# Two groups of unread products in the begin of an attention and two-layer kernel, where there were five

## The chip, the core and the metric

The kernel runs on one core of a Trainium2 chip. The metric is the device time of one execution in microseconds (us); smaller is better. The engines named below are TensorE (PE in the rows; PEld is its weight load), VectorE (DVE), ScalarE (ACT), GpSimd (POOL) and SyncE (SP), whose queue issues the loads and stores.

## The reference

Inputs are q, k, v of shape (4, 8, 768, 64), eight memory keys and values for each of the 32 heads, and four weight matrices. Attention goes by chunks of 32 queries: each chunk sees the 8 memory keys, 16 keys to the left of it, its own 32 and 8 to the right, 64 in all. The heads are then joined to 3072 tokens of 512 features, and two layers follow:

```python
scores = scale * np.matmul(q_c, k_full.transpose(0, 1, 3, 2))
a = np.exp(scores - max); a = a / (sum + 1e-09)
x = np.matmul(a, v_full)              # joined to (3072, 512)
h = x @ w_in;  g = h * np.clip(h + 3.0, 0.0, 6.0) / 6.0;  x = g @ w_out
h = x @ w_in2; g = np.maximum(0.01 * h, h);               out = g @ w_out2
```

Both layers have 2048 hidden features. The weights come as 64-bit floats and are decoded on the chip.

## The kernel before

**Arithmetic.** A float32 product is made from three products of a coarse float32r part and a remainder: coarse by coarse, remainder by coarse, coarse by remainder. So each operand is split once: ACT casts the coarse part (recorded as line 341), DVE subtracts it for the remainder (recorded as line 344).

**The begin.** The first block of 512 tokens needs the attention of two whole units of work, (0, 0) and (0, 1), which are 384 tokens by half the heads each, and of two half units, (1, 0, 0) and (1, 1, 0). One unit is a chain that goes from engine to engine: SP loads queries, keys and values; ACT, DVE or POOL copies the keys into windows (lines 525 and 795) and POOL the memory values (lines 517 and 789); PE makes the scores (line 544, halves 811); DVE finds the greatest (561 and 563, halves 825 to 834); ACT makes exponentials (580, halves 845); DVE sums and normalises (598, halves 862); PE transposes (602, halves 866); ACT copies the transposed weights back (recorded as 341); PE makes the values (622, halves 882 and 894); ACT and DVE split the result into xh and xl. Then come the products of the first layer, `hidden` (line 998) and `output` (line 1047), in groups of 12 products of 128x512, with half units (1, 0, 1) and (1, 1, 1) and later units between them. Beside all this the weights are decoded: ACT (396), then DVE (400, 404, 408), then split as above.

**Unread products.** `warm` (line 454) issues products of the identity matrix into a corner of a PSUM bank that no instruction reads. Each of its products shows as two records in the trace.

```python
def warm(n, after=None, home=None):
    b, c = home or Buf("ac"), 2 if home else 4
    def fn(e):
        x = made(b)[:, 1, N - 128 * c:].rearrange("p (a n) -> p a n", a=c)
        for _ in range(n):
            nc.tensor.matmul(x, ident, ident.unsqueeze(1).to_broadcast([128, c, 128]), start=True, stop=True, skip_group_check=True)
    add(fn, {"PE": c * n * (220.0 if after else 430.0)}, after.key + 0.5 if after else -200.0, after=[after] if after else [], allocs=[] if home else [b], uses=[home] if home else [], ins=4 * n)
```

Four groups stand among the first scores (lines 1560 to 1563). Line 1565 adds five more, each released by a mark: ("s", ...) is the scores of a unit, ("t", ...) its transposes, ("v", ...) its values. They write 256 columns each (128x256 in the rows) into `home`, the bank "ac" of the half unit (1, 1, 0). The exponentials of that half unit read the same bank, and instructions on one bank are kept in their order.

**The order of the work.** Nothing is written in the order in which it runs. A planner, `schedule` (line 103), holds a time for each engine and picks, whenever one is free, the ready task with the lowest key; the cost that a task names is the planner's time for it. The order that it finds is the program order of each engine's queue, and an engine takes its queue in order. For a group of two products with a home, the planner's PE cost is 2 x 2 x 220 = 880 ns, and its key lies 0.5 after that of its mark: -77.5, -86.5, -80.5, -68.5 and -67.5 for the five groups, against -80 for the values of unit (0, 0), -81 for the transposes of (0, 1), -74 for the values of (0, 1) and -68 and -62 for those of the half units.

**The loads.** SP issues loads in program order, at most eight outstanding; a ninth waits for the landing of the first (the kernel's planner counts the same eight, line 92). A load also waits until its buffer is free.

Of the kernel before, what the change touches and what calls it, by code (L numbers as in the profile page):

```python
# [255 lines left out]
def tile_attn_moe_moe2(ctx: ExitStack, tc: tile.TileContext, raw, w1i, w1o, w2i, w2o, out):  # L256
# [197 lines left out]
# [10 lines that stand above are left out]
# [1098 lines left out]
    warm(2, marks["s", 0, 1])  # L1562
    warm(1, marks["s", 1, 0, 0])
    home = marks["b", 1, 1, 0][0]
    for m, n in ((("s", 1, 1, 0), 2), (("t", 0, 0), 3), (("t", 0, 1), 3), (("t", 1, 1, 0), 2), (("v", 1, 0, 0), 2)):
        warm(n, marks[m], home)
    for u in range(2):
        half_unit(1, u, 1, -20.0 + 6.0 * u, "at", LOADS[4 + u], "ACT", 1.0)
# [45 lines left out]
    for kind, j, f, *n in seq2:  # L1614
        if kind == "p":
            p, i, n = j, f, n[0]
# [69 lines left out]
```

## Time and profile before

| | us |
|---|---|
| median of 3 runs | 1044.6 (1043.4 to 1045.1) |
| the profiled execution, its own time | 1042.63 |
| its span, first to last instruction | 1040.9 |
| PE busy | 1030.1 |
| DVE busy | 855.1 |
| ACT busy | 692.6 |

The profile is of one execution; 1.7 us of its time lie outside the span. A row of a timeline gives the start and the duration of merged neighbours on one engine, the line, the operation, what is written from what, the count, and in brackets the idle time ahead of it with what ended it.

### The profile page before, as it was taken

The numbers are of one execution on the slowest core, as the hardware profiler recorded it, in microseconds if no ns is written. First come the engines' busy times: TensorE is split into PE (matmuls) and PEld (weight loads), VectorE is DVE, ScalarE is ACT, GpSimd is POOL, SyncE is SP. The second block draws the span as 40 slices with busy tenths as digits, with TensorE's granted clock in tenths as the row PEclk, the third lists the DMA queues.
The fourth block names the chain that finished last, engine by engine and source line by source line (L and its number), as shares of the span: only waits on it lengthen the run. The fifth ranks groups of instructions, "written<-read, shape, count | busy, mean of one in ns | idle before, by whom it ended". The sixth has DMA issues, their size and how long they took to land.

```text
span 1040.9 us, 20153 instructions
## 1 busy us (share of the span) xinstructions
PE 1030.1 (99%) x7476; PEld 849.9 (82%) x7476; DVE 855.1 (82%) x1423; ACT 692.6 (67%) x1478; POOL 22.3 (2%) x30
## 2 busy tenths in 40 slices
PE   7999999999999999999999999999999999999998
PEld 4788988888888888888888888888888888888887
DVE  6896897578999887599999898999466998566775
ACT  4896776656888554576786576775565874666753
POOL 4010000000000000000000000000000000000000
PEclk9999999999999999999999999999999999999999
DMA  9889787887897989464638894456342564522451
GB/s 266 297 241 324 258 281 238 254 293 221 286 315 232 328 280 322 157 214 135 215 129 281 268 299 151 152 170 204 128 156 81 182 200 143 179 105 99 144 182 61
DMA packets 127315, 220.50 MB, mean 212 GB/s; under 512 B 12528, under 2 KB 76016, under 8 KB 127216
## 3 DMA queue, kind: packets, MB, share of 16 engines
q1 hardware_dynamic: 127216, 219.20, 63.1%
q8 instruction: 59, 0.97, 0.4%
q14 instruction: 40, 0.33, 0.1%
HBM read 156.24 MB, written 62.91 MB: 211 GB/s over the span
## 4 chain that ended last, share of the span: by engine, by line
PE 96%; DMA 1%; DVE 1%; ACT 1%; issue 0%; SPq 0%; ACTq 0%; DVEq 0%
PE y L1322 17%; PE y L1047 15%; PE y L1490 13%; PE h L1322 11%; PE h L1490 8%; PE hx L1490 8%; PE hx L1322 8%; PE h L998 8%; PE h L1047 2%; PE at L634 2%; DMA w<-in_raw 1%; PE at L544 1%; PE at L602 1%; PE ac L461 1%; ACT w L845 0%; PE at L622 0%
## 5 line engine op out<-in xcount | busy, mean ns | idle before, releaser
L344 DVE TENSOR_TENSOR w<-w 128x512 fp32r<-128x512 f32 (+2 forms) x407 | 333.4, 858 | 28.6 <-ACT w L341 28.2
L341 ACT CAST w<-w 128x512 fp32r<-128x512 f32 (+1 forms) x296 | 226.5, 799 | 16.6 <-DMA w<-floats 7.2
L1322 PE MATMUL y<-w 128*128 128x512 f32 x516 | 124.5, 390 | 0.0
L1047 PE MATMUL y<-g,w 128*128 128x512 f32 (+1 forms) x540 | 124.4, 374 | 0.0
L1322 PEld LDWEIGHTS y<-w 128*128 128x128 f32 x516 | 96.7, 188 | 19.9
L1047 PEld LDWEIGHTS y<-g,w 128*128 128x128 f32 x540 | 94.2, 189 | 17.3
L341 ACT CAST g<-w 128x512 fp32r<-128x512 f32 x80 | 49.7, 622 | 67.6 <-PE y L1490 22.3
L1490 PE MATMUL y<-w 128*128 128x512 f32 x384 | 90.3, 389 | 0.0
L1490 PEld LDWEIGHTS y<-w 128*128 128x128 f32 x384 | 72.1, 188 | 14.9
L1296 ACT ACTIVATE w<-w 128x512 f32<-128x512 f32 x72 | 45.2, 631 | 43.0 <-DVE w L1289 21.5
L344 DVE TENSOR_TENSOR g<-w,g 128x512 fp32r<-128x512 f32 x80 | 54.8, 694 | 14.6 <-ACT g L341 14.4
L998 PE MATMUL h<-xh,w 128*128 128x512 f32 (+1 forms) x288 | 66.0, 370 | 0.0
L1490 PE MATMUL h<-w 128*128 128x512 f32 x264 | 62.1, 389 | 0.0
L1490 PE MATMUL hx<-w 128*128 128x512 f32 x252 | 59.2, 389 | 0.0
L1322 PE MATMUL h<-xl,w 128*128 128x512 f32 x240 | 58.2, 390 | 0.0
L1490 PEld LDWEIGHTS h<-w 128*128 128x128 f32 x264 | 49.6, 188 | 10.2
L998 PEld LDWEIGHTS h<-xh,w 128*128 128x128 f32 x288 | 49.7, 189 | 8.9
L1490 PEld LDWEIGHTS hx<-w 128*128 128x128 f32 x252 | 47.3, 188 | 9.8
L1322 PEld LDWEIGHTS h<-xl,w 128*128 128x128 f32 x240 | 44.9, 188 | 9.3
L1322 PE MATMUL y<-xh,w 128*128 128x512 f32 x216 | 52.0, 390 | 0.0
L1367 DVE TENSOR_TENSOR w<-y,w 128x512 f32<-128x512 f32 x35 | 24.0, 691 | 29.7 <-PE y L1322 26.9
L1322 PEld LDWEIGHTS y<-xh,w 128*128 128x128 f32 x216 | 40.5, 188 | 8.4
(243 smaller groups left out, 1836.5 us busy)
## 6 DMA issues: line engine op xcount, KB each, us to landing
w<-kept2i SPq DMA_DIRECT2D x42, 512.0 KB
w<-kept2o SPq DMA_DIRECT2D x42, 512.0 KB
w<-kept1i SPq DMA_DIRECT2D x28, 512.0 KB
a<-in_raw SPq DMA_DIRECT2D x20, 448.0 KB
w<-in_w1i SPq DMA_DIRECT2D x16, 512.0 KB
w<-in_w1o SPq DMA_DIRECT2D x16, 512.0 KB
w<-in_w2i SPq DMA_DIRECT2D x16, 512.0 KB
w<-in_w2o SPq DMA_DIRECT2D x16, 512.0 KB
```

Source lines behind the costliest of these rows:

```text
L341: nc.scalar.copy(out, in_) if e == "ACT" else engine(e).tensor_copy(out=out, in_=in_)
L344: engine(e).tensor_tensor(out=out, in0=a, in1=b, op=ALU.subtract)
L461: nc.tensor.matmul(x, ident, ident.unsqueeze(1).to_broadcast([128, c, 128]), start=True, stop=True, skip_group_check=True)
L544: nc.tensor.matmul(ps.t[h * CHUNK:(h + 1) * CHUNK, par, i * W:(i + 1) * W], qk[h // 2].t[r, gp, (h % 2) * G + c * CHUNK:(h % 2) * G + (c + ...
L602: nc.tensor.transpose(pt.t[:, i // NC, (i % NC) * 128:(i % NC + 1) * 128], pview()[:, i * 128:(i + 1) * 128], ident)
L634: nc.tensor.matmul(pv.t[(h % 2) * D:(h % 2 + 1) * D, par, (h // 2) * 2 * G + i * CHUNK:(h // 2) * 2 * G + (i + 1) * CHUNK], v[h // 2].t[r, ...
L998: nc.tensor.matmul(h.t[:, o:o + n], w.t[:, 1 if p == 1 else 0, k * 128:(k + 1) * 128], x[:, k, c0:c0 + n], start=(p == 0 and k == 0 and o ...
L1047: nc.tensor.matmul(bank(banks[d])[:, c0:c0 + n], w.t[:, 1 if p == 1 else 0, d * 128:(d + 1) * 128], g.t[:, 1 if p == 2 else 0, at:at + n], ...
L1296: return add(lambda e: nc.scalar.activation(out=at(), in_=at(), func=AF.Prelu, alpha=0.01), {"ACT": act(N)}, key, after=[after], uses=uses)
L1322: nc.tensor.matmul(bank(to), wt(l, o)[:, kt * 128:(kt + 1) * 128].bitcast(F32R), operand(p, name, 1 if q == 2 else 0, kt).bitcast(F32R), s ...
L1367: done[2] = add(lambda e: nc.vector.tensor_tensor(out=half_of(x, 0), in0=bank(bb), in1=ut.t[:, 0], op=ALU.add), low, key, after=[k, done[1 ...
L1490: nc.tensor.matmul(bank(to[d]), wt(1 if q == 1 else 0, o)[:, d * 128:(d + 1) * 128].bitcast(F32R), g.t[:, 1 if q == 2 else 0], start=(fres ...
```

## The change

It takes three of the five groups of line 1565 out: the one behind the scores of half unit (1, 1, 0), the one behind its transposes, and the one behind the values of half unit (1, 0, 0). The two behind the transposes of the whole units stay, three products each.

```diff
-    for m, n in ((("s", 1, 1, 0), 2), (("t", 0, 0), 3), (("t", 0, 1), 3), (("t", 1, 1, 0), 2), (("v", 1, 0, 0), 2)):
+    for m, n in ((("t", 0, 0), 3), (("t", 0, 1), 3), ):
         warm(n, marks[m], home)
```

## Rows read from the trace of the kernel before

**Rows 1.** The page, part 1: busy us (share of the span) and instructions.
```profile
PE 1030.1 (99%) x7476; PEld 849.9 (82%) x7476; DVE 855.1 (82%) x1423; ACT 692.6 (67%) x1478; POOL 22.3 (2%) x30
```
**Rows 2.** Waits of PE over the span: in total, times, longest, us.
```profile
PE ac L461 <- ACT w L845: 2.0, 1, 2.0
...
PE at L602 <- DVE w L598: 1.2, 2, 0.9
```
**Rows 3.** Timeline of PE, 17 to 45 us: start, us, work, idle before.
```profile
17.50 0.84 PE L602 MATMUL at<-ident,w 128*128 128x128 f32 x6 [0.25 <-DVE w L598]
18.94 1.56 PE L461 MATMUL ac<-ident 128*128 128x256 f32 x6 [0.59 <-DVE mx L825]
22.47 1.13 PE L461 MATMUL ac<-ident 128*128 128x256 f32 x4 [1.97 <-ACT w L845]
23.53 2.92 PE L622 MATMUL at<-w 64*64 64x32 f32 x96
26.38 1.54 PE L602 MATMUL ab<-ident,w 128*128 128x128 f32 x6
27.72 2.77 PE L461 MATMUL ac<-ident 128*128 128x256 f32 x6
...
31.13 1.78 PE L622 MATMUL ab<-w 64*64 64x32 f32 x96
32.84 1.13 PE L461 MATMUL ac<-ident 128*128 128x256 f32 x4
...
34.81 1.13 PE L461 MATMUL ac<-ident 128*128 128x256 f32 x4
35.87 0.98 PE L882 MATMUL ac<-w 64*64 64x32 f32 x48
36.78 0.72 PE L811 MATMUL at<-w 64*32 64x64 f32 x48
37.44 2.11 PE L998 MATMUL h<-xh,w 128*128 128x512 f32 x8
...
44.34 1.14 PE L894 MATMUL at<-w 64*64 64x32 f32 x48 [0.61 <-ACT w L341]
```
**Rows 4.** Windows: length, busy us of PE, PEld, DVE, ACT, POOL, granted clock, DMA.
```profile
20.50:22.47 1.97, 0.00 (x1) 0.00 (x1) 1.71 (x3) 1.93 (x13) 1.89 (x2) 1.00 0.73 180
23.36:38.39 15.03, 15.03 (x368) 12.85 (x367) 11.72 (x29) 9.14 (x30) 2.88 (x4) 0.77 0.83 277
23.65:30.48 6.83, 6.83 (x109) 6.09 (x110) 5.41 (x10) 2.30 (x6) 2.59 (x4) 0.50 0.96 368
...
38.39:78.00 39.61, 38.96 (x398) 31.37 (x397) 39.15 (x80) 36.94 (x118) 2.97 (x2) 1.00 0.84 266
45.41:1037.30 991.89, 990.94 (x6726) 822.86 (x6723) 822.55 (x1337) 664.88 (x1378) 11.31 (x7) 1.00 0.63 210
```
**Rows 5.** Timeline of ACT, 18 to 62 us.
```profile
18.88 0.78 ACT L341 COPY w<-at 128x768 f32<-128x768 f32 x1
20.54 0.31 ACT L845 ACTIVATE w<-ac,mx 128x64 f32<-128x64 f32 x1 [0.88 <-PE ac L461]
...
35.42 1.14 ACT L341 COPY w<-w 128x336 f32<-128x336 f32 x4
...
61.51 2.23 ACT L341 COPY w<-w 128x336 f32<-128x336 f32 x8 [0.78 <-DMA w<-in_raw]
```
**Rows 6.** Timeline of DVE, 23 to 39 us: its two idle stretches.
```profile
27.58 1.15 DVE L344 TENSOR_TENSOR xl<-at,xh 128x256 fp32r<-128x256 f32 x4 [1.42 <-ACT xh L341]
...
32.42 0.43 DVE L400 TENSOR_SCALAR wm<-wm 128x512 uint32<-128x512 uint32 x1 [1.89 <-ACT wm L396]
```
**Rows 7.** Timeline of POOL, 14 to 16 us.
```profile
14.21 1.27 POOL L341 COPY w<-w 8x768 f32<-8x768 f32 x2 [1.88 <-DMA w<-in_raw]
```
**Rows 8.** Timeline of SP's queue, 33 to 34 us.
```profile
33.36 0.27 SPq L787 DMA_DIRECT2D w<-in_raw  x1
33.76 0.40 SPq L769 DMA_DIRECT2D w<-in_raw  x1
```

## The prediction, made before the changed kernel was run

> **What bounds the kernel now.** I read the page first. PE is busy for 1030.1 of 1040.9 us [rows 1], so the kernel is a chain of products with some 10 us of holes, and a change to a few products can only matter by what PE waits for or by how fast it runs. The waits of PE come next [rows 2]: its longest wait is one of 2.0 us, of an unread product (line 461) for the exponentials of line 845. After the begin there is next to nothing: from 45.41 us to the end PE idles 0.95 us (the last line of that group) [rows 4], one wait for the normalisation. So whatever the change does, it does before 45 us, and the rest follows as a block, sooner or later by what the begin gives.
>
> The timeline of PE through the begin [rows 3] shows where the groups stand. The six records at 18.94 us are the group behind the transposes of unit (0, 0), which stays. The four at 22.47 are the first group that goes. The six at 27.72 stay. The four at 32.84 and the four at 34.81 go. Between 23.53 and 43 us PE has no hole at all. That looks like a PE bound, but part of the work in it is unread, and part of it is slow: the table of stretches gives a granted clock of 0.50 from 23.65 to 30.48 us [rows 4], the lower of the two levels, 1.2 GHz instead of 2.4. It fell after PE had done nothing for 1.97 us (20.50 to 22.47).
>
> DVE is the other engine to watch. From 23.36 to 38.39 us it is busy for 11.72 of 15.03 us, so 3.31 us of it are idle, and from 38.39 to 78 us it is busy for 39.15 of 39.61 [rows 4]. Its two holes are of 1.42 and 1.89 us, and sum to just those 3.31 [rows 6]: the first waits for the split of unit (0, 0)'s values, the second for a decode that stands on ACT behind the copy of transposed weights. Both are late because PE is late.
>
> **The change part by part.** *The group at 22.47 us.* The values of unit (0, 0) follow it at 23.53. Their inputs are there long before: ACT has the transposed weights copied at 18.88 + 0.78 = 19.66 us [rows 5], POOL has the memory values of that unit at 14.21 + 1.27 = 15.48 [rows 7]. The group that stays ends at 20.50. So the values can begin at 20.5 instead of 23.53: 3.03 us, of which 1.97 are the wait and 1.06 the products. The group waits because the exponentials read the same bank from 20.54 on [rows 5], and everything behind it on PE's queue waits with it.
>
> *The slow stretch.* If PE goes on at 20.5 without a hole, the work of 23.53 to 30.48 runs at 2.4 GHz. The same 96 products of values take 2.92 us there and 1.78 us at 31.13; six transposes 1.54 against 0.84 at 17.50; six unread records 2.77 against 1.56 at 18.94 [rows 3]. That is 1.14 + 0.70 + 1.21 = 3.05 us.
>
> *The groups at 32.84 and 34.81 us.* They cost 1.13 us each, 2.26 together [rows 3], and the values of the half units come that much sooner.
>
> On PE alone that makes 3.03 + 3.05 + 2.26 = 8.3 us: the values of the second half unit would end at 28.5 instead of 35.87 + 0.98 = 36.85. But PE is not alone. The scores of half unit (1, 0, 1) at 36.78 need the key windows that ACT copies at 35.42 [rows 5], behind casts that wait for DVE; the first-layer products at 37.44 need the remainders of DVE. DVE can close its 3.31 us of holes and no more, since from 23.36 on it has that work before it whatever PE does, and it has no holes behind. ACT is busy for 9.14 of the same 15.03 us and follows. So the begin comes 3.3 us sooner, and the other 5 us turn into idle time of PE, between 28.5 and about 35.42 + 1.14 - 3.3 = 33.2 us: 4.7 us in which it has nothing to do.
>
> *What that idle time does to the clock.* After 1.97 us without work the clock fell [rows 4]; here are 4.7, and no unread product is left in them. I expect it to fall again. No row shows the price, so I bound it: nothing if it does not fall; 6.83 / 2 = 3.41 us if a stretch as long as the one in the trace lies wholly on first-layer products, which are on the path. A gain by the clock is excluded, because the real products behind run at full clock already. I take a stretch of that same length that starts halfway through the idle time, at 30.9 us: it ends at 37.7, has 4.5 us of real products in it, and costs half of that, 2.2 us.
>
> *The planner.* Three tasks of 880 ns leave its PE, and it may order later work otherwise. The nearest row says how little there is to lose or win, the 0.95 us that PE idles in all the rest [rows 4]; I take 0 and keep 1 us either way.
>
> The sum is -3.3 + 2.2 = **-1.1 us**. The profiled execution took 1042.63 us, 1.73 of them outside its span, and the sum says 1041.5 for it. It is 2.0 us below the median of the runs shown, 1044.6, to which I apply the same difference: **1043.5 us**. About 0.2%, 2.1 us, is what a measurement of this kernel can tell from no change, so my forecast is none that can be told.
>
> **A rule weighed against this.** Rows 4 show one fall of the clock in one execution, with its place. The Trainium skill, page "TensorE: Matmul & The Clock Gate", section "Part 1: The HAM clock gate", says that how many products run at the lower clock varies from run to run of the same kernel. By that rule the slow stretch of 23.65 us need not be in every execution of the kernel before, and the 3.05 us need not be there to win: the last rival below. The three times shown, all above the profiled one, neither show nor exclude it.
>
> **The rivals.**
>
> *The clock holds.* PE's idle time is shorter than I think, or cut up by the small products of the half units, and the clock stays at 2.4 GHz. For it: the hole of 0.59 us at 18.94 [rows 3] brought no fall, the clock stands at 1.00 behind it [rows 4]. Against it: the hole of 1.97 us brought one. Then the whole 3.3 us come through: 1044.6 - 3.3 = 1041.3 us.
>
> *The loads don't follow.* What SP issues behind 33.36 us is paced by landings: the next load of queries and keys goes out at 33.76, only 0.40 us later [rows 8], so an earlier free buffer moves it by at most 0.4 us. At 61.51 us ACT already waits 0.78 us for such a load [rows 5]; were everything else 3.3 us sooner, it would wait 4 us there, with casts that PE needs behind it. DVE and ACT are both over 93% busy in that stretch and could not make it up. Then 0.4 us are left: 1044.2 us. Against it: PE may have enough prepared work to bridge part of that wait, and the planner would put the copies later.
>
> *The fall moves from unread products to real ones (slower).* In executions of the kernel before without the slow stretch, its begin would already be 3.05 us sooner than in the profile, since PE's work up to 36.85 us, which DVE waits for, shrinks by that. The change can then win only 3.31 - 3.05 = 0.26 us, and pays for the fall that its idle time brings, 2.2 to 3.4 us: slower by 2.0 to 3.1, I take 2.5, 1047.1 us. It decides from the point where most executions of before lack the stretch and those of after have one on the first-layer products. For it: the group at 22.47 ends a hole, and the two at 32.84 and 34.81 fill just the place where the new hole would be. Against it: the only execution that can be seen has the stretch and is the fastest of the four times.
>
> *The change does nothing.* Unread products would be free if what follows them were not ready. At 22.47 us it is ready by 3 us, so I give this nothing of its own.
>
> **How the numbers follow.** My forecast, a gain partly paid back by the clock, gets 0.44; its bounds are 1041.3 and 1044.7. The clock holds: 0.22. The loads don't follow: 0.14. The fall moves to real products: 0.20. Faster by over 0.2% is the second case and the edge of the first, 0.22 + 0.03 = 0.25. Slower by over 0.2% is the last case without its mild end, 0.19. Within 0.2% is the rest, 0.56. The range goes from 1040.9, the second case with 0.4 for the planner, to 1047.0, near the middle of the last case; about 1 in 10 is left out above and less below.
>
> **What would show it.** In the timeline of PE the values of unit (0, 0) begin at 20.5 us right behind six unread records; the exponentials of line 845 no longer hold PE. In the stretches DVE is busy without a hole from 23.4 us to the scores of half unit (1, 0, 1), which come at about 33.5 instead of 36.78. PE idles some 4 us just before them, and the granted clock falls there and comes back among the products of line 998. The values at 44.34 us [rows 3] come 1 to 2 us sooner. I am wrong if the clock stays up through 29 to 40 us (then 3.3 us sooner), if PE has new waits between 45 and 80 us that end on ACT or a load (then the loads decide), or if the values of unit (0, 0) still begin at 23.5.

## The result, and the profile after

The changed kernel takes 1050.06 us (median of 6 runs, 1048.43 to 1051.58), the kernel before 1044.42 (6 runs, 1043.40 to 1046.29). The ratio is 1.0051, 95% interval 1.0038 to 1.0065: slower by 5.3 us, where no change was forecast and 1047.0 was the top of the range. Run again later it was slower by 0.41% (experiment 7). The profiled execution took 1048.93 us, its span 1047.2.

The page of the changed kernel, first lines:

```profile
span 1047.2 us, 20144 instructions
## 1 busy us (share of the span) xinstructions
PE 1028.2 (98%) x7464; PEld 845.8 (81%) x7464; DVE 854.1 (82%) x1421; ACT 694.0 (66%) x1478; POOL 24.8 (2%) x32
```

PE is busy for 1.9 us less than in [rows 1], and the span is 6.3 us longer. So 8 us more are idle. Where? Part of it is in the begin, as expected. The timeline of PE there, which answers to [rows 3]:

```profile
18.90 1.56 PE L461 MATMUL ac<-ident 128*128 128x256 f32 x6 [0.59 <-DVE mx L825]
20.39 0.82 PE L622 MATMUL at<-w 64*64 64x32 f32 x35
21.53 1.24 PE L622 MATMUL at<-w 64*64 64x32 f32 x61 [0.31 <-issue]
...
27.84 0.69 PE L882 MATMUL ac<-w 64*64 64x32 f32 x30
32.35 0.80 PE L882 MATMUL ac<-w 64*64 64x32 f32 x18 [3.82 <-issue]
34.24 1.46 PE L811 MATMUL at<-w 64*32 64x64 f32 x48 [1.09 <-ACT w L341]
35.63 3.14 PE L998 MATMUL h<-xh,w 128*128 128x512 f32 x8
```

The values of unit (0, 0) begin at 20.39, right behind the group that stays. Then PE stops for 3.82 us in the middle of the values of the second half unit, 30 records in, and waits for nothing that the profile shows ("issue"). A second wait, of 1.09 us, is for ACT. ACT makes the key windows of half unit (1, 0, 1) there, which it made at 35.42 in [rows 5]; the timelines of ACT and of SP's queue in the changed kernel:

```profile
33.58 1.11 ACT L341 COPY w<-w 128x336 f32<-128x336 f32 x4 [2.29 <-DMA w<-in_raw]
```

```profile
33.58 0.27 SPq L787 DMA_DIRECT2D w<-in_raw  x1
```

ACT had waited 2.29 us for the load of that half unit's queries and keys (line 769). The same landing lets SP's ninth load go, the row of SP; in the kernel before that row stands at 33.36 [rows 8]. So the load is no sooner than before, and it bounds the begin: the scores of (1, 0, 1) come 0.66 us behind the start of the copy, at 34.24 instead of 36.78. The copy begins as this load lands in experiments 1, 3, 5, 6 and 7 too (at 34.45, 33.16, 34.47, 33.47 and 33.70 us), and the scores 0.65 to 0.66 us behind it.

The first-layer products begin at 35.63 instead of 37.44. The scores before them take 1.46 us instead of 0.72, and the first eight products 3.14 instead of 2.11. The stretches of the changed kernel, columns as in [rows 4], say why these are slow, and where the rest of the time is:

```profile
28.53:32.35 3.82, 0.00 (x1) 0.00 (x0) 3.82 (x13) 1.82 (x7) 0.00 (x0) 0.83 0.99 317
31.03:37.86 6.83, 4.33 (x71) 3.37 (x71) 5.73 (x19) 4.49 (x18) 0.00 (x0) 0.50 0.68 184
...
45.00:1035.00 990.00, 983.44 (x6681) 814.10 (x6680) 819.11 (x1332) 664.94 (x1376) 13.95 (x9) 1.00 0.63 210
110.00:120.00 10.00, 8.13 (x125) 7.11 (x125) 9.97 (x18) 8.80 (x29) 1.65 (x1) 1.00 0.52 157
120.00:180.00 60.00, 56.79 (x923) 46.23 (x916) 50.46 (x99) 43.28 (x152) 3.04 (x2) 1.00 0.85 268
```

The clock stands at 0.50 from 31.03 to 37.86 us, on the scores and the first-layer products. But the larger part is behind the begin: from 45 to 1035 us PE idles 990.00 - 983.44 = 6.56 us, where the kernel before idles 0.95; 1.87 of it between 110 and 120 us, 3.21 between 120 and 180. The waits of PE behind 45 us in the changed kernel (total, times, longest):

```profile
PE at L544 <- issue: 2.3, 3, 1.8
PE y L1047 <- ACT g L341: 1.5, 1, 1.5
PE at L634 <- ACT a L341: 0.7, 1, 0.7
PE at L602 <- DVE w L598: 0.7, 1, 0.7
```

The kind of the last one is in [rows 2], but at another place (208.98 us there, 131.47 here); the others are not. They are of instructions that the change does not touch, in the attention units that run beside the first layer. The program itself is another there: set beside that of the kernel before, the changed kernel's differs in more than the three groups on all five engines, on ACT and DVE from 23 and 24 us and on PE from 44 to 346 us, since the planner, with three tasks less on its PE, picked another order. The timeline of PE at 150 us shows the kind of difference. First the kernel before, then the changed one:

```profile
157.35 1.62 PE L634 MATMUL at<-w 64*64 64x32 f32 x96
158.90 1.19 PE L998 MATMUL h<-xh,w 128*128 128x512 f32 x4
159.94 1.08 PE L998 MATMUL h<-xl,w 128*128 128x512 f32 x4
160.85 1.98 PE L1047 MATMUL y<-g,w 128*128 128x512 f32 x8
162.76 1.17 PE L544 MATMUL at<-w,a 64*32 64x64 f32 x96
```

```profile
152.09 1.62 PE L634 MATMUL at<-w 64*64 64x32 f32 x96
153.64 2.11 PE L1047 MATMUL y<-g,w 128*128 128x512 f32 x8
155.68 0.97 PE L544 MATMUL at<-w,a 64*32 64x64 f32 x72
158.47 0.43 PE L544 MATMUL at<-w,a 64*32 64x64 f32 x24 [1.82 <-issue]
```

In the kernel before, 16 products stand between the values of one unit (line 634) and the scores of the next (line 544). In the changed kernel it is 8, and PE stops inside the scores, again on "issue". The same distance of 8 comes five times in a row, at 122, 139, 156, 175 and 190 us.

What does PE wait for there? The DMA queues have one for instructions, q8. In the whole span of the changed kernel, then in the tenth of a microsecond from 156.00 and in the one from 29.60 (packets, MB, and the packet's whole time, 0.96 and 1.09 us, as a share of 16 engines in that stretch):

```profile
q8 instruction: 59, 0.97, 0.4%
```

```profile
q8 instruction: 1, 0.02, 60.1%
```

```profile
q8 instruction: 1, 0.02, 68.4%
```

59 packets of 16 KB are one for every 253 of PE's 14,928 products and weight loads. Between 142 and 173 us there are just two, at 156.0 and 159.7. Each stop of PE on "issue" of over 0.2 us behind 16 us ends 2.2 to 2.8 us after such a packet. There are 28 in the ten profiles, none of them in the kernel before. Thirteen, in the changed kernel and in experiments 1 to 3, 6 and 7, in us; the last column counts PE's records (products, weight loads and what its sequencer does besides) in order of their start, up to the one with which PE goes on:

```
kernel         PE stands        packet   packet to going on   record
changed         28.53 -  32.35   29.63    2.7              1218 =  4 x 256 + 194
changed        123.02 - 123.26  120.55    2.7              3778 = 14 x 256 + 194
changed        156.65 - 158.47  156.06    2.4              4803 = 18 x 256 + 195
experiment 1    28.10 -  32.62   30.11    2.5              1218 =  4 x 256 + 194
experiment 2   122.62 - 122.86  120.07    2.8              3779 = 14 x 256 + 195
experiment 2   138.91 - 140.01  137.57    2.4              4291 = 16 x 256 + 195
experiment 2   156.72 - 158.35  156.03    2.3              4802 = 18 x 256 + 194
experiment 3    30.01 -  31.71   29.22    2.5              1218 =  4 x 256 + 194
experiment 6    31.69 -  32.03   29.62    2.4              1218 =  4 x 256 + 194
experiment 7   121.93 - 122.22  119.96    2.3              3778 = 14 x 256 + 194
experiment 7   155.30 - 156.03  153.62    2.4              4803 = 18 x 256 + 195
experiment 7   173.56 - 173.79  171.36    2.4              5314 = 20 x 256 + 194
experiment 7   188.72 - 189.18  186.81    2.4              5826 = 22 x 256 + 194
```

The fifteen others, in the changed kernel and in experiments 1 and 4 to 8 (some of them ahead of large products), lie at 2.2 to 2.7. All 28 end at a record that is 194 or 195 over a multiple of 256, and the multiple is the number of the packet: before record 14 x 256 + 194 it is the 14th of the queue. A packet of 16 KB is thus a block of 256 instructions, and PE stands because the next block is not there yet. The traces have 570 such block starts; PE never begins a block sooner than 2.19 us after its packet, and most blocks come in time. The stops are 0.23 to 4.77 us long and the distance stays. Where two packets follow each other at such a place, they are 3.3 to 3.8 us apart (156.0 and 159.7 in the changed kernel; 137.7 and 141.0), while 96 small products take 1.62 us, so that 128, with their weight loads a packet's 256 instructions, take an estimated 2.2. Values and scores with only 8 products between them use instructions faster than they come. The Trainium skill says on its page "Runtime: NRT & Kernel Launch", section "Instruction fetch mechanics", that a sequencer fetches ahead in blocks of 16 KiB, 256 instructions, and that crossing a block is mostly hidden. The size agrees with the packets and the records; that it is hidden does not hold in these runs of small products.

All kernels of this study run the same 4272 products of the two layers in the same order, so the start of the n-th of them tells where one gains or loses on another. Starts in the profiled executions, the first column in us, the others as differences from it (the kernels of the last three columns are those of experiments 2, 1 and 5):

```
product   before   changed   products kept   order kept   units apart
   1       37.44    -1.81        +0.88          -0.95        -0.93
  13       40.29    -0.77        +0.88          +1.40        +0.19
 201       90.80    -1.06        +1.01          +1.73        +0.34
 336      111.96    -1.06        +1.02          +2.77        +1.11
 345      113.04    +1.22        +1.02          +2.76        +2.24
1301      363.53    +6.30        +6.43          +3.30        +2.86
4272     1036.96    +6.30        +6.43          +3.30        +2.86
```

The changed kernel is 1.06 us ahead at 112 us, about the gain that the prediction worked out, and loses 7.4 us between there and 360. The execution of before that was profiled, 1042.63 us, is among its shorter ones (27 later runs: 1042.28 to 1046.42, median 1044.18), so profile differences come out some 1.5 us larger than ratios of medians.

### The profile page after: what moved, and what is told of

The parts are those of the page before. It is cut to its first block, busy times and chain, and to the rows that moved or that the text cites. A ratio compares the mean times of both kernels' runs of the same rounds, so it can differ in the third digit from the quotient of the medians.

```text
span 1047.2 us, 20144 instructions
## 1 busy us (share of the span) xinstructions
PE 1028.2 (98%) x7464; PEld 845.8 (81%) x7464; DVE 854.1 (82%) x1421; ACT 694.0 (66%) x1478; POOL 24.8 (2%) x32
## 4 chain that ended last, share of the span: by engine, by line
PE 86%; DMA 6%; DVE 3%; ACT 2%; SPq 2%; issue 1%; POOL 0%; DVEq 0%; ACTq 0%; POOLq 0%
PE y L1322 15%; PE y L1490 12%; PE y L1047 12%; PE h L1322 10%; PE h L1490 8%; PE hx L1322 8%; PE hx L1490 8%; PE h L998 6%; DMA w<-in_raw 3%; PE h L1047 2%; PE at L634 2%; DMA w<-in_w1i 1%; PE at L544 1%; DMA half<-ys 1%; DMA w<-in_w1o 1%
## 5 line engine op out<-in xcount | busy, mean ns | idle before, releaser
L341 ACT CAST g<-w 128x512 fp32r<-128x512 f32 x80 | 49.6, 621 | 76.3 <-PE y L1047 23.4
```

Of the source, the lines that this page charges most:

```text
L341: nc.scalar.copy(out, in_) if e == "ACT" else engine(e).tensor_copy(out=out, in_=in_)
```

## The experiments

Two theories stood against each other. A: the time is lost by the planner's other order behind the begin. B: it is lost because the products are gone, by idle PE and the lower clock on real products, which was the prediction's rival on the slower side. Each experiment gave 6 to 12 timed runs, beside 27 of before in experiments 1 to 4, and 29 in 5 to 8.

**1. The order kept, the products gone** (e1_held). The three groups stay tasks of the planner but issue nothing. Every other engine's program is that of the kernel before, instruction for instruction.

```diff
...
-            for _ in range(n):
+            for _ in range(n if issue else 0):
...
-        warm(n, marks[m], home)
+        warm(n, marks[m], home, issue=n == 3)
```

> The three groups stay tasks of the planner, with their costs and keys, but issue no product: every engine's program is that of the kernel before, less the three groups. Theory A (the time is lost to the other order that the planner writes behind the begin): the begin goes as in the changed kernel, 0 to 2 us sooner, the rest as before: 1042.5 to 1044.5 us, no PE wait over 1 us between 45 and 340 us. Theory B (it is lost because the products are gone: idle PE and the lower clock on first-layer products): as the changed kernel, 1049 to 1051 us.

Measured: 1045.09 us, ratio 1.0006 (0.9997 to 1.0016). With the order of before, taking the products away costs nothing that can be told. The longest PE wait behind 45 us is 0.9 us. Theory B falls as the main cause; theory A's range is missed by 0.6 us. The begin did not win, though: PE's stop on "issue" among the values of the second half unit is 4.51 us here, the clock is low for 10.2 us from 31.3, and the table shows 1.40 us lost at product 13.

**2. The products kept, the order changed** (e2_unseen). The groups are issued, at no cost in the planner. ACT, DVE, POOL and SP have exactly the programs of the changed kernel.

```diff
...
-        add(fn, {"PE": c * n * (220.0 if after else 430.0)}, ...
+        add(fn, {"PE": c * n * (220.0 if after else 430.0) * seen}, ...
...
-        warm(n, marks[m], home)
+        warm(n, marks[m], home, seen=n == 3)
```

> The three groups are issued, but cost the planner nothing: DVE, ACT, POOL and SP have the programs of the changed kernel, PE too, plus the three groups. Theory A: slow as the changed kernel or a little more, 1049 to 1052 us, with PE waits behind 100 us. Theory B: as before, 1043.5 to 1045.5 us.

Measured: 1047.68 us, ratio 1.0031 (1.0017 to 1.0045). The order alone makes the kernel slower, clearly out of theory B's range, but by less than theory A had said: 3.2 us, of the 4.3 to 5.3 of the whole change. Its waits of PE between 120 and 180 us are of the same kinds and in the same places as those of the changed kernel:

```profile
PE at L544 <- issue: 3.1, 4, 1.6
PE at L602 <- DVE w L598: 0.5, 1, 0.5
```

In these profiles the scores of line 544, from the start of each product to that of the next, take 17.3 us here and 16.7 in the changed kernel, against 13.2 in the kernel before. The products of line 1322 take 2.2 us more in both, most of it at 283, 287 and 335 us, the later two ahead of waits of PE for ACT (0.7 and 0.4 us); no distance of 8 stands there.

The table tells a second thing. The begin of this kernel is 2.1 us later than the changed one's at product 336, and 0.2 us earlier at 345: a begin that was sooner gained nothing here. In the changed kernel PE waits at 112.68 us for a cast of ACT, and ACT itself had waited for the landing of a store that frees a buffer (line 396, timeline of ACT in the changed kernel):

```profile
104.44 1.27 ACT L396 ACTIVATE ys<-w 128x512 f32<-128x512 f32 x2 [3.64 <-DMA half<-ys]
```

That wait is 1.14 us in the kernel before and ends at 102.98. SP's queue was 0.7 us later in the changed kernel, at the loads of 90 us, although PE was 1.1 us sooner.

**3. Only the first group gone** (e3_first_gone), **4. only the last two gone** (e4_last_two_gone). The planner makes an order of its own for each.

```diff
-    for m, n in ((("s", 1, 1, 0), 2), (("t", 0, 0), 3), (("t", 0, 1), 3), (("t", 1, 1, 0), 2), (("v", 1, 0, 0), 2)):
+    for m, n in ((("t", 0, 0), 3), (("t", 0, 1), 3), (("t", 1, 1, 0), 2), (("v", 1, 0, 0), 2)):
```

```diff
-    for m, n in ((("s", 1, 1, 0), 2), (("t", 0, 0), 3), (("t", 0, 1), 3), (("t", 1, 1, 0), 2), (("v", 1, 0, 0), 2)):
+    for m, n in ((("s", 1, 1, 0), 2), (("t", 0, 0), 3), (("t", 0, 1), 3)):
```

> Only the group behind the scores of the half unit is left out; the planner sees it gone and writes an order of its own. Theory B: the hole at 20.5 us is closed and the two later groups still fill PE: 2 to 3 us faster than before, 1041.5 to 1042.5 us. Theory A: the begin gains as much, but the time goes by the waits behind 45 us that this order happens to have: anywhere from 1042 to 1050 us, the sum of those waits over the 0.95 us of before explaining it to within 1 us.

> Only the two groups behind the transposes and values of the half units are left out; the planner writes an order of its own. Theory B: the wait at 22.47 us stays, and the slow clock falls on unread products or small ones: 1044 to 1047 us. Theory A: again anywhere from 1042 to 1050 us by the waits behind 45 us, and the differences of this run and of the one with only the first group gone do not add up to that of the whole change.

Measured: 1044.19 us, ratio 0.9998 (0.9987 to 1.0008), and 1048.32 us, ratio 1.0042 (1.0027 to 1.0057). Theory B's gain of 2 to 3 us in the first does not come: the products of the first layer begin 2.24 us sooner, the clock falls there (33.5 to 40.3 us), and at product 13 nothing is left. The second is slow by one wait, at 113.86 us, which brings the clock down for 3.4 us too (timeline of PE, and a stretch of it):

```profile
113.86 2.08 PE L1047 MATMUL y<-g,w 128*128 128x256 f32 x8 [2.53 <-ACT g L341]
```

```profile
113.28:116.69 3.41, 2.83 (x13) 2.83 (x14) 3.41 (x5) 1.73 (x5) 1.46 (x1) 0.50 0.49 112
```

So an order can lose its time in more than one place: this one has the distance of 8 only once, at 122 us, and 16 or more elsewhere up to 200 us. The claim that the waits explain each run to within 1 us was too bold: in the first the profile is 2.0 us behind that of before, with 0.6 us more of idle PE behind 45 us. As for adding up: by the ratios -0.2 and 4.4 us give 4.2, which the whole change's 4.3 to 5.3 do not contradict; that part of the expectation missed.

**5. The units held apart** (e10_apart). If the distance from values to scores is what the other order loses by, restoring it must bring the time back, with the products still gone.

```diff
...
                     tag = blocked(t)
+                    if progress < since + t.gap:
+                        held.append(item)
+                        continue
...
                 pick.fn(e)
+                since = progress if pick.ends_unit else since
...
+        t.gap = 4.0 if j > 2 else 0.0
```

> The changed kernel, and the planner holds the scores of a later unit (j of 3 and more) back until 16 products lie behind the values of the unit before it, as in the order of the kernel before; in the changed kernel it is 8. Theory C (the other order loses its time because scores follow values too closely, and PE then runs out of code, and ACT and DVE out of time): the waits of PE between 120 and 180 us that end on issue, ACT or DVE fall from 3.2 to under 1 us, and the time comes back to 1044 to 1046.5 us. Rival D (any other order costs as much; the units' distance is not it): 1048 to 1051 us.

Measured: 1045.28 us, ratio 1.0012 (1.0001 to 1.0024). From 1.0041 and 1.0051 this is back to within 0.12%, inside what theory C said. The stretch of 120 to 180 us has 0.15 us of idle PE instead of 3.21, and the waits behind 45 us are these (lines are shifted by the edit, 544 is 550 and 1047 is 1055):

```profile
120.00:180.00 60.00, 59.85 (x907) 49.56 (x908) 50.28 (x100) 42.78 (x141) 4.88 (x3) 1.00 0.87 276
```

```profile
PE y L1055 <- DVE g L350: 0.7, 2, 0.4
PE at L608 <- POOL w L604: 0.7, 1, 0.7
PE y L1055 <- issue: 0.5, 1, 0.5
PE y L1055 <- ACT g L347: 0.4, 1, 0.4
```

No stop on "issue" in the scores is left. What stays, 0.12%, is near that of experiment 1, and the interval nearly reaches no change.

**6. The later groups doubled, the order kept** (e6_doubled). To see what the products do in the begin, the first group issues nothing and the other two issue four products each.

```diff
...
-            for _ in range(n):
+            for _ in range(n if issued is None else issued):
...
-        warm(n, marks[m], home)
+        warm(n, marks[m], home, n if n == 3 else 4 * (m[0] != "s"))
```

> The order of the kernel before on every engine; the group behind the scores of the half unit issues nothing, those behind the transposes and the values of the half units issue four products instead of two. Theory E (in the begin the clock and PE's code are what is lost when the groups go): no wait on issue before the scores of half unit (1, 0, 1), the clock stays at full rate through the first-layer products, which begin 1.5 to 2.5 us sooner than in the kernel before and keep it to 45 us. Then, if a sooner begin carries through, 1042 to 1043 us; if the loads set the pace further on, the lead is gone by 115 us and the time is 1043.5 to 1045 us. Without theory E: a hole and the lower clock in the first-layer products as in the run with only the first group gone, 1044 to 1045 us.

Measured: 1045.07 us, ratio 1.0008 (0.9995 to 1.0021). Half a hit, and 0.07 us above both of the ranges that were left. The stop on "issue" among the values shrinks to 0.34 us:

```profile
32.03 0.72 PE L882 MATMUL ac<-w 64*64 64x32 f32 x33 [0.34 <-issue]
```

It is 4.51 us with none of the three groups (experiment 1), 1.70 with the later two as they were (experiment 3), and not over 0.2 with all in the kernel before. But the first-layer products begin only 0.12 us sooner than in the changed kernel with its stop of 3.82 us: PE still idles 1.37 us before the scores of half unit (1, 0, 1), for the copy that waits for the load. The clock falls at 34.6 us for 3.4, and the lead of 1.93 us is 0.76 at product 13. By 102 us it is -0.11, gone, as the loads' case said. So this stop did not bound the begin.

**7. The changed kernel again** (e9_after_again).

> The changed kernel once more, on the chip of the other three. If the missing products themselves cost some 2 us in this order, as the first runs have it (ratio 1.0051 here, 1.0031 with the products issued): 1049 to 1051 us. If they cost nothing and the first difference was chance: 1046.5 to 1048.5 us.

Measured: 1048.40 us, ratio 1.0041 (1.0026 to 1.0057). This lies in the second of the two ranges, near its top. Beside experiment 2 (1.0031, up to 1.0045) the missing products would cost 1 to 2 us in this order, but the intervals overlap: that they cost anything is not shown. Its profile has the same waits in the same places: on "issue" in the scores at 122.2, 156.0, 173.8 and 189.2 us.

**8. All five groups, another cost** (e5_cost_660). Nothing is removed; the planner counts three quarters of the cost for the three groups.

```diff
...
-        add(fn, {"PE": c * n * (220.0 if after else 430.0)}, ...
+        add(fn, {"PE": cost * c * n * (220.0 if after else 430.0)}, ...
...
-        warm(n, marks[m], home)
+        warm(n, marks[m], home, cost=1.0 if n == 3 else 0.75)
```

> All five groups are issued as before, but the planner counts 660 ns for each of the three instead of 880, and writes another order, in which scores still lie 16 or more products behind values up to 200 us. Theory C: 1043.5 to 1046 us. Rival D (any other order costs): 1047 to 1051 us.

Measured: 1043.60 us, ratio 0.9999 (0.9988 to 1.0009). Another order, and no loss: rival D, that any other order costs, falls, and theory C gets its second hit. It is a mild test, since PE's own order is that of the kernel before up to 137 us and only ACT's and DVE's differ from 34 us on. No version beat the kernel before.

## Why the prediction was wrong

**The step that failed is the planner's.** The prediction took 0 for the new order and kept 1 us either way, by the 0.95 us that PE idles behind the begin in the kernel before. That row says how little the present order has to lose. It does not say what another order may cost, and was no bound for it. Experiment 2 measures the term with the products in place, +0.31% (0.17 to 0.45), about 3.2 us; experiment 5 takes most of the whole loss back by one constraint on the order. So the order as the cause is shown. For the distance between units the evidence is weaker: two orders that have 8 five times in a row are slow (the changed kernel and experiment 2), and three others that keep 16 or more are not (experiments 3, 5 and 8). But experiment 4 has 8 only once and is as slow, by a wait for ACT at 113.86 us, and some 2 us of the loss in the first two lie near 287 and 335 us, away from any such place. That the stops on "issue" are waits for instructions is shown by the count of records, 28 stops of 28, though no run changed how instructions are fetched. What part of the 3.2 us each kind of wait makes stays open: the stops are some 2 to 3 us in the profiles, the rest are waits for ACT and DVE.

**The begin's sum was nearly right, its terms less so.** The values of unit (0, 0) came at 20.39, forecast 20.5. The clock fell at 31.03 and came back at 37.86, forecast 30.9 to 37.7. PE idled 4.9 us ahead of the scores, in two pieces with 18 values between them, forecast 4.7. But the scores of (1, 0, 1) came 2.54 us sooner, not 3.3. The bound was not DVE's holes: DVE's timeline has none from 23.4 us to the start of the scores, and the scores waited for ACT's copy and that for a load, which landed no sooner than before. The landing stood in rows 8, at 33.36; the prediction read from it when the next loads go out, and not that the copy needs it. PE's stop for instructions, which no row of before could show, cost the begin little: with a stop of 0.34 us instead of 3.82 the first products come 0.12 us sooner (experiment 6). The lower clock cost 0.74 us on the scores and 1.03 on the first eight products, 1.77 where 2.2 was taken. So 2.54 - 1.77 = 0.77 us were left at product 13, for a forecast of 1.1: both terms were too large, and their errors cancel in part. That the table has -1.06 at product 201 is luck; in between it is -1.83, at product 100. With the order of before the same begin gave no gain (experiment 1: +0.06%, -0.03 to 0.16).

**The rivals.** "The loads don't follow" had its mechanism right, and sooner than it thought: a load bounds the scores at 33.58 us, and the lead of 1.06 us is lost at 112 us to a wait that goes back over ACT to a store's landing, where it had named ACT's wait for a load at 61 us. "The fall moves to real products" happened and cost 1.8 us, where its price had 2.2 to 3.4; that executions of the kernel before lack the slow stretch, its other half, no profile of that kernel shows. Its sign was right for another reason. "The clock holds" did not happen. Of the signs of being wrong none came: the prediction looked for new waits between 45 and 80 us, and they lay behind 110. The rule of the Trainium skill that was weighed (page "TensorE: Matmul & The Clock Gate", section "Part 1: The HAM clock gate"), that the number of slow products varies between runs of one kernel, can't be tested on the one profile of the kernel before. The changed kernel has two, with nearly the same stretch (31.03 to 37.86 us, and 30.93 to 37.76 in experiment 7); the kernel of experiment 8, which issues all five groups as well, had no slow stretch behind 18 us.

## What to carry to other kernels

Where a planner turns costs into program order, a task that is taken out, even one that does nothing, changes the program everywhere behind it; price that by what other orders cost, not by the idle time of the present one, or hold the order fixed and change one thing. Keeping the task and issuing nothing separates the two in one run. And look at the queue of instructions where small products follow each other: large products between them, even unread ones, give the next block time to come. In the begin here that bought nothing, because a load came last; before pricing a begin, look for the landing that each copy on its path needs.

## What was not expected of the hardware

PE ran out of instructions inside runs of small products (48 or 96 of 64x32 or 64x64, each with its weight load): in the begin for 4.51 us with none of the later two groups' products issued and for 0.34 us with eight, in the same order (experiments 1 and 6), and up to 1.82 us in the scores at 158 us. It does so at the border of a block of 256 instructions, and goes on 2.2 to 2.8 us after the block's packet goes out. A packet never went out sooner than 43 records before PE began the block ahead of it, so no more than some 300 instructions were sent for ahead of PE. In the begin a packet went out later, in four of the profiles 1.1 to 2.4 us after PE had already stopped (in the changed kernel at 29.63 us, with the DMA engines 99% busy). Why it was late there is not shown. The same kernel stood for 1.82 us in those scores in one execution and 0.72 in another (experiment 7), so such a stop varies between runs. And a sooner begin carried through only in part: of leads of 0.9 to 2.2 us at the first product, 0.8 us were left at the end in the profile of experiment 8, and nothing in the others.
